# Loads and stores over 128 partitions in one transfer each, and another order of the first transfers, in a fused H3 and feed-forward kernel

## The chip, the cores and the metric

The kernel runs on one core of one Trainium2 chip. The metric is the device time of the whole program in microseconds, the median of several executions. The profile is of one execution; a span is the time from its first to its last instruction.

## The reference

For x of 2048 rows by 576 columns in float32, with xn the rows of x made zero-mean and unit-variance, the output is the sum of three parts:

```
xn  = (x - mean(x)) / sqrt(var(x) + 1e-5)
kv  = conv4(k, shift_k) * v                     # four taps along the sequence, causal, by channel
y   = causal_conv(kv, ssm_k) + kv * ssm_D       # 2048 taps, by channel; the reference goes by an FFT
out = x + xn * y + relu(xn @ w1) @ w2           # w1: 576 x 4608, w2: 4608 x 576
```

k and v are 2048 x 576, shift_k 576 x 4, ssm_k 576 x 2048, ssm_D 576. Everything is float32.

## The kernel before, in words

**Tiles.** A sequence position is p * 32 + u * 16 + t, with p below 64, u below 2, t below 16. Tile t holds 128 positions, one in each partition u * 64 + p, so a tile of x, k, v or out is two runs of 64 rows, each with a fixed step in DRAM, and the step from one run to the other differs. The function `move` (line 157) copies such a tile with one transfer for each u, over 64 partitions each. x is taken in pairs of tiles t, t+1, which lie next to each other in DRAM: 4608 bytes for each partition (`load_acc`, tile `acc`; a pair doubles as the accumulator of the output rows).

**Feed-forward part.** Four tiles are a block of 512 rows; there are four blocks. The hidden size is cut into 18 pairs of 128 columns. Matmuls are done in a rounded float32 (`F32R`), each operand split into a high and a low part and three of the four products summed. The columns of w1 come by `load_w1` into `both_w1` (named both_w in the profile): four groups of 128 rows, and the last 64 rows twice, in both halves of the partitions. `split_plain` and `split_rest` split them into `g` tiles; the high part is a copy on ACT (line 469), the low part a subtraction on POOL (line 431). w2 comes by `load_w2` into r (two buffers) and is split into w (line 531). Blocks 0 and 1 run against all pairs first, with plain products (`mm1`, line 569), then blocks 2 and 3 with a scheme of fewer products (`quad`, line 545). `unit` (line 632) multiplies by w2 and adds into acc.

**Opening.** `first_xT` centres the four tiles of block 0, tiles 0 and 2 on DVE (lines 179 to 200), tiles 1 and 3 on ACT (lines 254 and 256), transposes them on TensorE (line 262) and splits them into b1, b2 and xr (lines 221 to 227). Until then `keep_warm` runs matmuls on zeros (line 1112).

**Conv part.** `conv` is a generator; `tick`, called between the matmuls of the feed-forward part, advances it by its share. Its stages: the transform of ssm_k; that of kv, for which k and v are loaded two tiles ahead by `move` and the taps run on DVE (line 818 and around); a middle stage in DRAM tiles; and the output stage, which loads x again (tile xt), multiplies by it and, for the first eight tiles, stores to out from POOL's queue. The other eight tiles are stored from SP's queue out of acc (line 160), the last of them in halves (line 645).

**Order.** A scheduler lays out each engine's instructions from the program and its constraints (`issue_after`, `here`); each engine then runs its own in that order, and a waiting one holds those behind it. Transfers are issued from three queues: SP (q1 in the profile), ACT (q10) and POOL (q0).

Of the kernel before, what the change touches and what calls it, by code (L numbers as in the profile page):

```python
# [17 lines left out]
P = 128  # L18
# [22 lines left out]
NG = A1 // GR  # L41
N_WARM = 21
WARM_TILE = (0, 10, 0, 2)

# [65 lines left out]
def h3_ffn_kernel(ctx: ExitStack, tc, x, k, v, shift_k, ssm_k, ssm_D, w1, w2, fwd, inv, mid, out):  # L110
# [42 lines left out]
    def halves(u):  # L153

        return slice(u * A1, (u + 1) * A1), slice((1 - u) * A1, (2 - u) * A1)

    def move(tile_, rows, t, store=False, queues=(nc.sync, nc.sync)):
        for u in range(U):
            a, b = tile_[halves(u)[0]], rows[u, :, t]
            queues[u].dma_start(*((b, a) if store else (a, b)))  # L160

    pairs = {}

    def load_x(t, tag, bufs, late=False, **queues):
        pair = xp.tile([P, 2, D], F32, tag=tag, name=f"acc{t}", bufs=bufs)
        if late:
            with here():
                nc.vector.memset(pair[:, :, :1], 0.0)
        move(pair, x, slice(t, t + 2), **queues)
        return pair  # L170

    def load_acc(t, **queues):
        pairs[t] = load_x(t, f"acc{place(t // BT)}", BT // 2, **queues)
        acc[t], acc[t + 1] = pairs[t][:, 0, :], pairs[t][:, 1, :]
# [63 lines left out]
    def first_xT(srcs):  # L238
# [8 lines left out]
        for t in range(BT):  # L247
            xn = rows[t]
            if t % 2 == 0:
                with tc.issue_after(behind.ins) if behind else nullcontext():  # L250
                    stats(t, srcs[t])
                    behind = centred(xn, srcs[t], t)
            else:
                nc.scalar.activation(xn, srcs[t], AF.Copy, scale=-1.0 / D,
                                     accum_out=neg[:, t:t + 1])
                done["act"] = nc.scalar.activation(xn, srcs[t], AF.Identity,
                                                   bias=neg[:, t:t + 1])
                with tc.issue_after(done["act"].ins):
                    (split_plain if t == 1 else split_rest)(0, 0)
            for c in range(5):  # L260
                w = min(P, D - c * P)
                nc.tensor.transpose(ps[c][:w, t * P:(t + 1) * P], xn[:, c * P:c * P + w], ident)
            keep_warm(WARM_TILE[t])
        for c in range(5):
            last = split_low(c, ps[c], place(0))
            if c == 1:
                with tc.issue_after(last.ins):
                    split_plain(0, 1)
        with tc.issue_after(done["dve"].ins):
# [167 lines left out]
    def load_w1(n):  # L437
        f0 = (n % NPAIR) * FC
        r1 = both_w1[:, 5:] if n < NPAIR and n % 2 else both_w1
        for o, step in ((0, P), (P, FC - P)) if n == 0 else ((0, FC),):  # L440
            f, to = slice(f0 + o, f0 + o + step), slice(o, o + step)
            queue = nc.gpsimd if n == 0 and o == 0 else nc.sync
            queue.dma_start(r1[:, :4, to], w1[:4 * P, f].rearrange("(c p) f -> p c f", p=P))
            for h in range(2):
                queue.dma_start(r1[64 * h:64 * h + 64, 4, to], w1[4 * P:, f])
        raw_w[n] = r1
        weights[n] = {}
# [18 lines left out]

    def split_into(n, hi, lo, src):
        with at_turn(n):
            nc.scalar.activation(hi, src, AF.Copy)  # L469
        split_lo(lo, src, hi)  # L470

    def split_plain(n, j):
        g = weights[n][j] if j in weights[n] else group(n, j)
        weights[n][j] = g
        split_into(n, g[:, 0], g[:, 1], raw_w[n][:, :4, j * P:(j + 1) * P])

# [83 lines left out]
    def mm1(n, s, j):  # L560
# [3 lines left out]
        for c in range(4):  # L564
            b = ops[s, "b2" if c % 2 else "b1"][:, :, c // 2]
            seq += [(g[:, 0, c], b[:, 0]), (g[:, 0, c], b[:, 1]), (g[:, 1, c], b[:, 0])]
        seq += rest(n, j, s)
        for i, (a, m) in enumerate(seq):
# [46 lines left out]
    def unit(ns, s, b, i, h, last):  # L615
# [27 lines left out]
        if final and t == T - 1:  # L643
            for u, queue in ((0, nc.sync), (1, nc.scalar)):
                queue.dma_start(out[u, :, t, dc], acc[t][halves(u)[0], dc])
        elif last and h:
# [50 lines left out]
    def conv():  # L697
# [5 lines left out]
        with hold_pool as kp:  # L703
# [14 lines left out]
            def load(t):  # L718
                win[t] = slot(WIN + t % (KS + 1))
                if t >= 0:  # L720
                    move(win[t], k, t, queues=(nc.sync, nc.sync))
                    gates[t] = slot(GATE + t % 2)
                    move(gates[t], v, t, queues=(nc.sync, nc.sync))
                else:
# [257 lines left out]
        with tc.tile_pool(name="fo", bufs=2) as fp:  # L982
# [37 lines left out]
            def add(i):  # L1020
                if i >= 0:
# [5 lines left out]
                    if t < HT:  # L1027
                        move(to, out, t, store=True, queues=(nc.gpsimd, nc.gpsimd))
                    else:
                        added.add(t)  # L1030
# [70 lines left out]
    nc.vector.memset(warm, 0.0)  # L1101
    for t in range(0, BT, 2):
        load_acc(t, queues=(nc.sync, nc.scalar))
    load_w1(0)
# [14 lines left out]
    with tc.issue_after(done["act"].ins):  # L1119
        split_rest(0, 1)  # L1120
    load_w1(1)
    for t in range(BT, HT, 2):
        load_acc(t)
    for h in range(2):
        load_w2(0, h)
    for j in range(FT):
# [127 lines left out]
```

## Time and profile before

| | |
|---|---|
| median of 3 runs | 1058.05 us (1057.59 to 1059.14) |
| the profiled execution's own time | 1057.93 us |
| its span | 1056.2 us |
| TensorE busy | 1047.1 us, 99% of the span |
| DVE, ACT, POOL busy | 70%, 52%, 38% |
| moved by DMA | 204.45 MB, mean 194 GB/s |
| chain that ended last | PE 97%, DVE 1%, DMA 1% |

A row of the profile's groups or timeline has the start or the count, the engine, the line, the operation, output<-input and shapes; the part behind the bar or in brackets is idle time ahead of it and what ended it. A queue's row has its packets, MB, and the time of its packets as a share of sixteen DMA engines' time. A row of DMA issues has output<-input, the issuing queue, the count, KB of one and the median microseconds from issue to landing.

### The profile page before, as it was taken

The page shows a single profiled execution, that of the slowest core. Times are in us where ns is not written, and L with a number is a line of the kernel's source. Part 1 is how long each engine was busy: PE and PEld are TensorE (multiplying, and loading weights), DVE is VectorE, ACT ScalarE, POOL GpSimd, SP SyncE. Part 2 cuts the span into 40 slices and gives each one's busy share as a digit, 9 for nine tenths or more (in the row PEclk, how much of TensorE's full clock was granted, in tenths as well). Part 3 has the DMA queues.
Part 4 walks back from the last instruction along what each step waited for, and adds up shares of the span by engine and source line. Part 5 has one row for each costly group of instructions (what it writes and reads, how often), then busy time and mean ns, then how long its engine had stood idle before and what let it go on. Part 6 is the DMA issues. An engine that isn't in the chain of part 4 may idle for free.

```text
span 1056.2 us, 20042 instructions
## 1 busy us (share of the span) xinstructions
PE 1047.1 (99%) x7153; PEld 988.2 (94%) x7153; DVE 743.9 (70%) x1316; ACT 550.7 (52%) x1201; POOL 398.2 (38%) x398
## 2 busy tenths in 40 slices
PE   8999999999999999999999999999999999999998
PEld 5889999999999999999999999999999999999997
DVE  5539778787776788773477887778877773666664
ACT  5226566534343444433277787687777773444341
POOL 4133333333222333352443534343433444544641
PEclk9999999999999999999999999999999999999999
DMA  9944867777566766755876655656555648776864
GB/s 230 205 98 134 226 172 209 201 227 212 151 191 178 212 177 197 239 164 187 277 219 193 192 173 166 195 172 197 167 177 175 183 127 264 221 228 214 287 191 113
DMA packets 156304, 204.45 MB, mean 194 GB/s; under 512 B 32846, under 2 KB 122704, under 8 KB 155181
## 3 DMA queue, kind: packets, MB, share of 16 engines
q1 hardware_dynamic: 143308, 189.00, 60.5%
q0 software_dynamic: 12576, 13.44, 5.6%
q8 instruction: 56, 0.92, 0.4%
q10 hardware_dynamic: 320, 0.74, 0.3%
q14 instruction: 44, 0.35, 0.1%
HBM read 133.92 MB, written 55.05 MB: 179 GB/s over the span
## 4 chain that ended last, share of the span: by engine, by line
PE 97%; DVE 1%; DMA 1%; ACT 0%; issue 0%; SPq 0%; DVEq 0%
PE pso L632 43%; PE psh L569 22%; PE psb L545 14%; PE psf L907 7%; PE psa L545 6%; PE psf L687 3%; PE psf L1051 1%; PE psf L1053 1%; DMA acc<-in_x 1%; DVE bn L179 0%; PE psf L278 0%; ACT hh L551 0%; DVE lok L897 0%; DVE acc L641 0%; DVE yl L932 0%
## 5 line engine op out<-in xcount | busy, mean ns | idle before, releaser
L632 PE MATMUL pso<-w,hh 128*128 128x288 f32 x2304 | 468.9, 295 | 1.6 <-ACT w L531 0.8
L632 PEld LDWEIGHTS pso<-w,hh 128*128 128x128 f32 x2304 | 372.5, 188 | 9.8 <-ACT w L531 1.2
L632 PE MATMUL pso<-w,ll 128*128 128x288 f32 x1152 | 329.5, 295 | 0.0
L431 POOL TENSOR_TENSOR g<-both_w,g 128x256 fp32r<-128x256 f32 (+2 forms) x145 | 168.4, 1167 | 374.1 <-ACT g L469 322.4
L569 PE MATMUL psh<-b,g 128*128 128x512 f32 x864 | 218.2, 395 | 0.5 <-ACT b L226 0.2
L632 PEld LDWEIGHTS pso<-w,ll 128*128 128x128 f32 x1152 | 213.3, 188 | 1.1
L569 PEld LDWEIGHTS psh<-b,g 128*128 128x128 f32 x864 | 156.9, 188 | 30.5 <-DVE b L227 0.5
L641 DVE TENSOR_TENSOR acc<-pso,acc 128x288 f32<-128x288 f32 x232 | 101.7, 450 | 61.9 <-PE pso L632 59.1
L431 POOL TENSOR_TENSOR w<-r,w 128x576 fp32r<-128x576 f32 x72 | 113.0, 1570 | 53.8 <-ACT w L531 53.7
L551 ACT ACTIVATE hh<-psh 128x512 fp32r<-128x512 f32 x72 | 42.9, 597 | 143.8 <-PE psh L569 143.8
L552 DVE SCALAR_TENSOR_TENSOR ll<-psh,hh 128x512 fp32r<-128x512 f32 x72 | 49.4, 687 | 69.8 <-ACT hh L551 69.3
L545 PE MATMUL psb<-t,g 128*128 128x256 f32 x648 | 94.9, 280 | 0.1
L545 PEld LDWEIGHTS psb<-t,g 128*128 128x128 f32 x648 | 85.5, 188 | 0.4 <-DVE psa L600 0.3
L469 ACT ACTIVATE g<-both_w 128x256 fp32r<-128x256 f32 (+2 forms) x145 | 76.3, 543 | 9.9 <-PE psb L545 6.6
L498 POOL TENSOR_TENSOR both_w<-both_w 128x256 f32<-128x256 f32 x72 | 62.8, 891 | 30.3 <-DMA both_w<-in_w 29.0
L545 PE MATMUL psa<-b,g 128*128 128x256 f32 x432 | 63.1, 280 | 0.0
L551 ACT ACTIVATE hh<-psa 128x512 fp32r<-128x512 f32 x36 | 21.5, 598 | 72.9 <-PE psa L545 72.7
L545 PE MATMUL psb<-b,g 128*128 128x256 f32 x432 | 57.5, 281 | 0.0
L545 PEld LDWEIGHTS psa<-b,g 128*128 128x128 f32 x432 | 56.6, 188 | 0.0
L545 PEld LDWEIGHTS psb<-b,g 128*128 128x128 f32 x432 | 54.4, 188 | 0.2
L950 DVE TENSOR_TENSOR k<-psf,k 128x288 f32<-128x288 f32 x64 | 29.0, 454 | 35.1 <-ACT sw L949 33.3
L673 POOL DMA_DIRECT2D wx<-in_fwd x32 | 17.6, 551 | 95.3 <-PE psf L687 85.6
(135 smaller groups left out, 1695.3 us busy)
## 6 DMA issues: line engine op xcount, KB each, us to landing
r<-in_w SPq DMA_DIRECT2D x72, 288.0 KB, 4.0
zy<-vo SPq DMA_DIRECT2D x64, 288.0 KB, 2.9
zo<-zy SPq DMA_DIRECT2D x32, 576.0 KB, 4.4
both_w<-in_w SPq DMA_DIRECT2D x35, 512.0 KB, 4.2
zk<-zk SPq DMA_DIRECT2D x64, 144.0 KB, 2.6
ztk<-zk SPq DMA_DIRECT2D x32, 288.0 KB, 3.4
ztx<-zx SPq DMA_DIRECT2D x32, 288.0 KB, 3.5
k<-k SPq DMA_DIRECT2D x64, 144.0 KB, 3.3
```

The lines of the kernel that those rows point to most:

```text
L431: return nc.gpsimd.tensor_tensor(dst, src, hi, OP.subtract)
L469: nc.scalar.activation(hi, src, AF.Copy)
L498: nc.gpsimd.tensor_tensor(dst, a, b, op)
L545: done["pe"] = nc.tensor.matmul(ps, a, m, start=start and i == 0, stop=i == len(seq) - 1, skip_group_check=not start)
L551: done["act"] = nc.scalar.activation(hh, ps, AF.Relu)
L552: lows.append(nc.vector.scalar_tensor_tensor(ll, ps, 0.0, hh, op0=OP.max, op1=OP.subtract))
L569: done["pe"] = nc.tensor.matmul(ps, a, m, start=i == 0, stop=i == len(seq) - 1)
L632: done["pe"] = nc.tensor.matmul(ps[:, :NH], a, m, start=c == 0, stop=c == len(seq) - 1)
L641: done["acc"] = nc.vector.tensor_tensor(acc[t][:, dc], ps[:, :NH], acc[t][:, dc], OP.add)
L687: nc.tensor.matmul(ps[:, :NH], w[:, n, :], stk, start=n == 0, stop=n == 1)
L907: nc.tensor.matmul(ps[:, :NH], a, m[:, cols], start=n == 0, stop=n == 2)
L950: nc.vector.tensor_tensor(k1[:, cols], ps, k1[:, cols], OP.mult)
```

## The change

`move` makes one transfer of a whole tile: the tile's 128 partitions on one side, `rows[:, :, t]` with u and p as its two outer dimensions on the other. The last 64 rows of w1 come by one transfer too, from a source that names them twice. The first pair of x is issued from ACT's queue, the second from SP's; the first tile of w1 from both of these in halves and no longer from POOL. Its high part is split after both centrings on ACT, and the second tile's high part is copied on POOL. The loads of w2 for pair 0 are issued ahead of block 1's x. There are 23 warm-up matmuls where there were 33, and the first twelve matmuls of block 0 take another order. The last tile's stores are split by columns, not by partitions.

```diff
-N_WARM = 21
-WARM_TILE = (0, 10, 0, 2)
+N_WARM = 20
+WARM_TILE = (0, 2, 0, 1)
...
-    def move(tile_, rows, t, store=False, queues=(nc.sync, nc.sync)):
-        for u in range(U):
-            a, b = tile_[halves(u)[0]], rows[u, :, t]
-            queues[u].dma_start(*((b, a) if store else (a, b)))
+    def move(tile_, rows, t, store=False, queue=nc.sync):
+        a, b = tile_, rows[:, :, t]
+        done["move"] = queue.dma_start(*((b, a) if store else (a, b)))
...
-                with tc.issue_after(done["act"].ins):
-                    (split_plain if t == 1 else split_rest)(0, 0)
+                if t == BT - 1:
+                    with tc.issue_after(done["act"].ins):
+                        split_plain(0, 0)
...
-            if c == 1:
+            if c == 2:
                 with tc.issue_after(last.ins):
-                    split_plain(0, 1)
+                    split_rest(0, 0)
+        split_plain(0, 1, nc.gpsimd.tensor_copy)
...
-            queue = nc.gpsimd if n == 0 and o == 0 else nc.sync
-            queue.dma_start(r1[:, :4, to], w1[:4 * P, f].rearrange("(c p) f -> p c f", p=P))
-            for h in range(2):
-                queue.dma_start(r1[64 * h:64 * h + 64, 4, to], w1[4 * P:, f])
+            cuts = ((nc.scalar, 0, 2), (nc.sync, 2, 4)) if n == 0 and o == 0 else ((nc.sync, 0, 4),)
+            for queue, a, b in cuts:
+                queue.dma_start(r1[:, a:b, to],
+                                w1[a * P:b * P, f].rearrange("(c p) f -> p c f", p=P))
+            nc.sync.dma_start(r1[:, 4, to], w1[4 * P:, f][None].to_broadcast([2, 64, step]))
...
+        if n == 0 and s == place(0):
+            seq = [seq[i] for i in (0, 3, 1, 2, 6, 4, 5, 9, 7, 8, 10, 11)]
...
-            for u, queue in ((0, nc.sync), (1, nc.scalar)):
-                queue.dma_start(out[u, :, t, dc], acc[t][halves(u)[0], dc])
+            (nc.scalar if h else nc.sync).dma_start(out[:, :, t, dc], acc[t][:, dc])
...
-                    move(win[t], k, t, queues=(nc.sync, nc.sync))
+                    move(win[t], k, t)
                     gates[t] = slot(GATE + t % 2)
-                    move(gates[t], v, t, queues=(nc.sync, nc.sync))
+                    move(gates[t], v, t)
...
-                        move(to, out, t, store=True, queues=(nc.gpsimd, nc.gpsimd))
+                        move(to, out, t, store=True, queue=nc.gpsimd)
...
-    for t in range(0, BT, 2):
-        load_acc(t, queues=(nc.sync, nc.scalar))
+    for t, queue in ((0, nc.scalar), (2, nc.sync)):
+        load_acc(t, queue=queue)
...
+    for h in range(2):
+        load_w2(0, h)
     for t in range(BT, HT, 2):
         load_acc(t)
-    for h in range(2):
-        load_w2(0, h)
```

SP's queue at the start, before and then in the changed kernel. acc0, acc2, acc4 and acc6 are the pairs of x (0 and 2 of block 0, 4 and 6 of block 1), both_w1 is w1, r2_n_h is half h of w2 for pair n; the shape is that of the written side.

```order
L160 DMA acc0_97<-in_x 64x1152
L160 DMA acc2_100<-in_x 64x1152
L443 DMA both_w1_94<-in_w1 128x4x128
L445 DMA both_w1_94<-in_w1 64x128 x2
L443 DMA both_w1_94<-in_w1 128x4x256
L445 DMA both_w1_94<-in_w1 64x256 x2
L160 DMA acc4_229<-in_x 64x1152 x2
L160 DMA acc6_232<-in_x 64x1152 x2
L452 DMA r2_0_0_235<-in_w2 128x2x288
L452 DMA r2_0_1_237<-in_w2 128x2x288
```

```order
L445 DMA both_w1_94<-in_w1 128x2x128
L159 DMA acc2_99<-in_x 128x1x1152
L447 DMA both_w1_94<-in_w1 128x1x128
L445 DMA both_w1_94<-in_w1 128x4x128
L447 DMA both_w1_94<-in_w1 128x1x128
L445 DMA both_w1_94<-in_w1 128x4x256
L447 DMA both_w1_94<-in_w1 128x1x256
L454 DMA r2_0_0_215<-in_w2 128x2x288
L454 DMA r2_0_1_217<-in_w2 128x2x288
L159 DMA acc4_219<-in_x 128x1x1152
L159 DMA acc6_221<-in_x 128x1x1152
```

Half of the first w1 tile now stands ahead of x's second pair on SP, w2 of pair 0 ahead of block 1's x. In both, two loads of ssm_D, w1 of pairs 2 and 3 and then r2_1_0 follow; ACT's queue holds the two other halves of x before, and acc0 and the other half of the first w1 tile in the changed kernel.

SP's queue in the transform of kv, a stretch with the loads of one tile (k and v are inputs, both the area they land in, xs and zx the conv's own transfers):

```order
L160 DMA both_345<-in_k 64x576 x2
L160 DMA both_345<-in_v 64x576 x2
L867 DMA zx_85<-both_345 128x288
L414 DMA kept_xr_93<-rows2_679 128x512
L867 DMA zx_85<-zx_2226 128x288
L841 DMA xs1_0_2897<-both_345 64x576
L841 DMA xs1_1_2898<-both_345 64x576
```

```order
L159 DMA both_329<-in_k 128x1x576
L159 DMA both_329<-in_v 128x1x576
L873 DMA zx_85<-both_329 128x288
L415 DMA kept_xr_93<-rows2_660 128x512
L873 DMA zx_85<-zx_2198 128x288
L847 DMA xs1_0_2864<-both_329 64x576
L847 DMA xs1_1_2865<-both_329 64x576
```

The order is the same; two transfers became one for k and one for v. The end of SP's queue, the stores of the last eight tiles:

```order
L160 DMA out_0<-acc8_6146 64x1152 x2
L160 DMA out_0<-acc10_6200 64x1152 x2
L160 DMA out_0<-acc12_5879 64x1152 x2
L160 DMA out_0<-acc14_5927 64x576 x2
L645 DMA out_0<-acc14_5927 64x288 x2
```

```order
L159 DMA out_0<-acc8_6073 2x64x1152
L159 DMA out_0<-acc10_6126 2x64x1152
L159 DMA out_0<-acc12_5809 2x64x1152
L159 DMA out_0<-acc14_5856 2x64x576
L651 DMA out_0<-acc14_5856 2x64x288
```

Each pair of stores is one, and the last tile's two SP stores are one, its second columns going from ACT.

More of the change, by code (lines that the diff above doesn't have):

```diff
@@ L155, in halves, with load_x @@
         return slice(u * A1, (u + 1) * A1), slice((1 - u) * A1, (2 - u) * A1)
-    def move(tile_, rows, t, store=False, queues=(nc.sync, nc.sync)):
-        for u in range(U):
-            a, b = tile_[halves(u)[0]], rows[u, :, t]
-            queues[u].dma_start(*((b, a) if store else (a, b)))
+    def move(tile_, rows, t, store=False, queue=nc.sync):
+        a, b = tile_, rows[:, :, t]
+        done["move"] = queue.dma_start(*((b, a) if store else (a, b)))
     pairs = {}
-    def load_x(t, tag, bufs, late=False, **queues):
+    def load_x(t, tag, bufs, late=False, **queue):
         pair = xp.tile([P, 2, D], F32, tag=tag, name=f"acc{t}", bufs=bufs)
@@ L168, in load_x, with load_acc @@
                 nc.vector.memset(pair[:, :, :1], 0.0)
-        move(pair, x, slice(t, t + 2), **queues)
+        move(pair, x, slice(t, t + 2), **queue)
         return pair
-    def load_acc(t, **queues):
-        pairs[t] = load_x(t, f"acc{place(t // BT)}", BT // 2, **queues)
+    def load_acc(t, **queue):
+        pairs[t] = load_x(t, f"acc{place(t // BT)}", BT // 2, **queue)
         acc[t], acc[t + 1] = pairs[t][:, 0, :], pairs[t][:, 1, :]
@@ L465, in group, with split_into, split_plain @@
         return wp.tile([P, 2, 4, P], F32R, tag="g", name=f"g{n}_{k}", bufs=4)
-    def split_into(n, hi, lo, src):
+    def split_into(n, hi, lo, src, copy=None):
         with at_turn(n):
-            nc.scalar.activation(hi, src, AF.Copy)
+            if copy:
+                copy(hi, src)
+            else:
+                nc.scalar.activation(hi, src, AF.Copy)
         split_lo(lo, src, hi)
-    def split_plain(n, j):
+    def split_plain(n, j, copy=None):
         g = weights[n][j] if j in weights[n] else group(n, j)
         weights[n][j] = g
-        split_into(n, g[:, 0], g[:, 1], raw_w[n][:, :4, j * P:(j + 1) * P])
+        split_into(n, g[:, 0], g[:, 1], raw_w[n][:, :4, j * P:(j + 1) * P], copy)
     def rest_flat(n):
```

## The prediction

> **What bounds the kernel now.** I read the page's busy times first, then the busy times by stage, then the queues and the DMA issues of each stage. TensorE is busy from the first microsecond to the last few:
>
> ```profile
> span 1056.2 us, 20042 instructions
> ...
> PE 1047.1 (99%) x7153; PEld 988.2 (94%) x7153; DVE 743.9 (70%) x1316; ACT 550.7 (52%) x1201; POOL 398.2 (38%) x398
> ...
> q1 hardware_dynamic: 143308, 189.00, 60.5%
> q10 hardware_dynamic: 320, 0.74, 0.3%
> ...
> 0.00:62.00 62.00, 57.95 (x312) 45.96 (x313) 28.84 (x75) 21.49 (x42) 18.40 (x23) 1.00 0.82 194
> 62.00:198.00 136.00, 136.00 (x822) 123.89 (x821) 103.84 (x194) 75.22 (x171) 47.41 (x56) 1.00 0.65 174
> 198.00:446.00 248.00, 248.00 (x1489) 225.32 (x1487) 193.12 (x307) 99.69 (x199) 76.26 (x75) 1.00 0.70 199
> 500.00:550.00 50.00, 50.00 (x386) 49.47 (x385) 26.98 (x53) 25.00 (x57) 19.02 (x20) 1.00 0.84 266
> 580.00:876.00 296.00, 295.91 (x2261) 292.09 (x2260) 230.74 (x402) 221.80 (x497) 120.62 (x103) 1.00 0.59 175
> 876.00:1041.00 165.00, 165.00 (x1267) 162.89 (x1266) 102.52 (x194) 65.51 (x151) 83.25 (x92) 1.00 0.72 224
> 1041.00:1056.00 15.00, 10.24 (x77) 9.91 (x75) 5.35 (x12) 0.60 (x1) 0.00 (x0) 0.98 0.60 157
> ```
>
> In the stage rows the columns are length, busy time of PE, PEld, DVE, ACT, POOL, granted clock, DMA share and GB/s. So what a change wins outside the opening and the last store must come off TensorE's own work, and this one takes none off. What it can lose is another matter: the last columns say that the sixteen DMA engines are already 0.59 to 0.84 busy. The conv's matmuls stand in TensorE's one queue between those of the feed-forward part, so a conv transfer that is late holds everything.
>
> **How a transfer is spread over engines.** The queue rows tell it. ACT's queue (q10) carries four transfers: two of 64 rows of x, two of 64 rows of out, 256 pieces. Its row has 320 packets, 64 more: each transfer closes with 16 packets, one for each engine. SP's program has 800 transfers that come to 130,559 pieces; with 16 closing packets each that is 143,359. The row has 143,308, which is 51 fewer. Five transfers are not of 64 or more rows: two loads over one row (ssm_D) and three over 63 (k, line 726). One engine for a single row is 15 fewer, twice, and nine engines of seven rows for 63 is 7 fewer, three times: 30 + 21 = 51. So engines are given equal shares of the outermost count; 63 rows use nine engines, not sixteen unevenly.
>
> In the changed kernel the DRAM side of every load of x, k and v and of every store of out is `rows[:, :, t]`, whose outermost dimension is u, of count 2; the tile's side has 128. The last 64 rows of w1 become a broadcast whose outermost count is 2 also. Equal shares on both sides at once are possible for two engines only. By the tile's side alone it would be sixteen; the transfers of before with unlike sides (32 against 128 rows, 256 against 128) have 16 in common and don't decide. I take two, and, as the simplest deal, one from the first engine on, the same two each time, so that all these transfers queue there.
>
> [...]
>
> **What a byte costs on one engine.** Two stretches bound it, one in which the output stage loads 128-row pieces and one in which block 1's x is loaded by halves:
>
> ```profile
> q1 hardware_dynamic: 189, 0.80, 99.8%
> q1 hardware_dynamic: 293, 1.08, 104.2%
> ```
>
> The first is 879 to 881 us: 0.80 MB / (2.0 us x 16 x 0.998) = 25 GB/s for an engine. The second is 12.5 to 17 us: 1.08 / (4.5 x 16 x 1.042) = 14.4 GB/s. I take 25, because two engines that draw 50 GB/s together are nearer to engines that nothing else slows; 14.4 is the other end. A pair of x tiles, 295 KB to each of two engines, is then 11.8 us, k or v of one tile 5.9 us, the rest of a w1 load 2.6 us.
>
> **The opening.** Until the second pair's w2 (r2_1_0 in SP's order) one engine of the two has, on its rings: four x pairs 4 x 295, the first w1 tile 16, its rest and the second tile 33 + 16 + 33, w1 of pair 1 33 + 66, two halves of w2 37, w1 of pairs 2 and 3 2 x 98, r2_1_0 itself 18: 1.63 MB. At 25 GB/s that is 65 us, from a start near 2 (the first x issue) to 67, plus 0.7 for the split of w2. Now:
>
> ```profile
> 0.76 1.23 ACTq L160 DMA_DIRECT2D acc<-in_x  x2
> 1.21 8.66 PE L1112 MATMUL psw<-warm 128*128 128x512 bf16 x33 [1.21 <-DVE table L1106]
> 9.36 0.63 ACT L469 ACTIVATE g<-both_w 128x512 fp32r<-128x512 f32 x1 [1.59 <-DMA both_w<-in_w]
> 9.82 0.82 DVE L179 BATCH_NORM_STATS2 bn<-acc 128x6 f32<-128x288 f32 x2 [2.01 <-DMA acc<-in_x]
> 10.07 1.28 POOL L431 TENSOR_TENSOR g<-both_w,g 128x512 fp32r<-128x512 f32 x1 [6.39 <-ACT g L469]
> 13.28 0.50 PE L569 MATMUL psh<-b,g 128*128 128x512 f32 x1 [0.25 <-ACT b L226]
> 26.00 0.69 ACT L531 ACTIVATE w<-r 128x576 fp32r<-128x576 f32 x1
> 30.32 0.69 PE L632 MATMUL pso<-w,hh 128*128 128x288 f32 x4
> ```
>
> The split at 26.00 is that of r2_1_0, and the matmuls that need it start at 30.32. They come at 68 instead: +38 us. The first real matmul (13.28), with x whole near 27, would be late by 16, which lies inside the 38. That w2 is issued ahead of block 1's x spares pair 0 the 24 us of those two loads; pair 1's w2 still stands behind them, on SP's queue, with w1 of pairs 2 and 3 behind x as well. At 14.4 GB/s the opening is 113 us long, +85.
>
> The other parts of the opening edit are covered by this wait: ten fewer warm-up matmuls, the g split behind the centring, the cast of the second tile on POOL (nearest row 10.07: 1.28 us for a 128x512 subtraction there), the new order of twelve matmuls. None of them can be read in the end time while x is late; with x early they cost what the first rival below charges.
>
> **The conv of x, 198 to 446 us.**
>
> ```profile
> both<-in_k SPq DMA_DIRECT2D x35, 144.0 KB, 4.5
> both<-in_v SPq DMA_DIRECT2D x30, 144.0 KB, 3.2
> both_w<-in_w SPq DMA_DIRECT2D x18, 64.0 KB, 3.5
> rows<-in_x SPq DMA_DIRECT2D x4, 288.0 KB, 4.1
> ```
>
> Of the 35, 32 are moved (the other three keep their 64 rows). Moved: 62 x 144 + 18 x 64 + 4 x 288 KB = 11.5 MB, 29 us of each of sixteen engines now and 230 us of each of two after. All traffic now takes 0.70 x 248 = 174 us of an engine; 174 - 29 + 230 = 375, against 248: +127. The taps wait for k within the same tile, so the load can't be put off past the stage. If part of the 0.70 is packets held up by each other and 25 GB/s is the whole price, 199 x 248 / 16 / 25 = 123 takes the place of 174, the load is 324 and the stage +76.
>
> **Block 2's x, 500 to 550 us.** Eight halves of x (the rows are the issues at 517 and 540 us) and four rests are 2.6 MB, 52 us in place of 6.6 on top of 0.84 x 50 = 42: 88, +38 if all is awaited there and 0 if the slacker stretch behind it takes it up. I take +25, since acc waits for them directly. In 62 to 198 us (four halves of x rows and eight rests, 1.7 MB) the load becomes 88 + 30 = 118 of 136, and in 580 to 876 (eighteen rests) 175 + 21 of 296: nothing in either.
>
> **The output stage and the last stores, 876 to the end.**
>
> ```profile
> xt<-in_x SPq DMA_DIRECT2D x32, 144.0 KB, 3.8
> out<-y POOLq DMA_DIRECT2D x16, 144.0 KB, 4.5
> both_w<-in_w SPq DMA_DIRECT2D x10, 64.0 KB, 4.8
> out<-acc SPq DMA_DIRECT2D x6, 288.0 KB, 3.5
> 1041.30 10.36 SPq L160 DMA_DIRECT2D out<-acc  x8
> 1051.75 1.43 SPq L645 DMA_DIRECT2D out<-acc  x2
> ```
>
> With the single tile and the last halves, out<-acc is 2.4 MB and the moved part on SP and ACT 7.7 MB: 19 us now, 155 after. 0.72 x 165 + 0.60 x 15 = 128 now; 128 - 19 + 155 = 264 of 180: +83. That holds the tail, where the last stores alone, 3 x 11.8 + 5.9 + 5.9 = 47 us of one engine, start at 1041 and have nothing behind which to hide. POOL's stores of y, if on the same two engines, add 41; I leave them out, as another queue.
>
> **The sum.** 38 + 127 + 25 + 83 = 273. The profiled execution is 1057.93 us, its span 1056.2; 1057.9 + 273 = 1331. That execution is 0.1 below the median of the three runs, 1058.05, so the forecast is 1330.
>
> **Rivals.** *Sixteen engines all the same* (the tile's 128 rows decide): then the change does what it says. For it: the two halves share one set of engines now, and the output stage's 128-row loads run at 399 GB/s where block 1's x runs at 240. The x pairs and the half of the first tile ahead of them, 1.31 MB, then take 3.3 to 5.5 us from 2, so x is whole at 5.3 to 7.5 in place of 9.8, and 23 warm-up matmuls end at 1.2 + 23/33 x 8.66 = 7.2. The first matmul comes 2.3 to 4.5 us sooner, less 0.6 for the first tile's split, which now follows the centring on ACT (row 9.36), and TensorE carries that to the end: 2.8 in the middle, 1055.2. Against it: 63 rows on nine engines. [...]
>
> *Two engines, but others each time*: each transfer is long, none queues. x 11.8 us, the opening +5; k lands 8 us after issue where 4.5 was, 2.5 late at each of 16 tiles, +40; the last pair's store +7. 1110. Nothing in the rows ties a transfer to an engine, nor the reverse.
>
> *Two engines at 14.4 GB/s*: the opening +85, the conv 174 - 29 + 400 = 545, +297, the rest twice its sum, +220: about 1660. For it the second rate row; against it that sixteen engines drew that together.
>
> **How the numbers follow.** Forecast 0.70, sixteen engines 0.12, changing engines 0.10, the slow rate 0.08. The forecast's own range is 1225 (38 for the opening, 76 for the conv, 0 for block 2, and 54 for the end by the same reckoning: 168) to 1480 (POOL's stores on top, and stalls in which the two engines run dry between tiles, some 100); the whole range reaches down to 1100 and up to 1500. A measurement of this kernel tells 0.2%, 2.1 us, from no change. Faster by that is 0.6 of the first rival, 0.07; same 0.04; slower 0.89.
>
> **What would show it.** Right: q1 has 140,710 packets (130,943 pieces and 9,767 closings, two for each of the 101 moved transfers) and q10 532; x is whole near 27 us; DVE waits for DMA on k in the conv; TensorE's busy share falls to near 80%, and the DMA share sinks while the span grows; the out stores end some 40 us after the last matmul. Wrong: 142,124 packets on q1, 560 on q10 and x landing before 9 us say sixteen engines; x near 14 us says two that change; 1600 says the rate.

## The result: 27% slower, and the profile after

The changed kernel takes 1340.75 us (median of 5 runs, 1337.87 to 1342.3) against 1058.05: a ratio of 1.2667, 95% interval [1.2649, 1.2684]. The forecast was 1330, its range 1100 to 1500. The profiled execution is the median one, its span 1339.0.

Rows of the page of the changed kernel (engines, then queues with packets, MB and share of sixteen engines' time):

```profile
span 1339.0 us, 19867 instructions
...
PE 1102.0 (82%) x7143; PEld 1032.6 (77%) x7143; DVE 743.4 (56%) x1316; ACT 549.9 (41%) x1200; POOL 390.6 (29%) x388
...
q1 hardware_dynamic: 140710, 189.19, 46.1%
q0 software_dynamic: 15888, 13.14, 4.4%
...
q10 hardware_dynamic: 532, 0.87, 0.2%
```

Both packet counts are those of two engines, to the packet (140,710 and 532; sixteen would have been 142,124 and 560). SP's queue moves what it moved before, 189 MB, and its packets take 46.1% of a longer span: 9,876 us of engine time, where 60.5% of 1056.2 was 10,224. By these figures the engines do no more work than before; by the packets it lies on fewer of them.

Where the time went is read by following the same matmul through both traces. Behind the warm-up each has 7,120 matmuls, and but for 18 places among the first 96, where the order was changed, they come in the same order; the n-th of one answers to the n-th of the other. The boundaries that the prediction used fall in the changed kernel at 107.4, 251.8, 599.0, 665.6, 779.8 and 1075.4 us, and the last matmul ends at 1299.4. Busy times by stage there (length, busy PE, PEld, DVE, ACT, POOL, granted clock, DMA share, GB/s):

```profile
0.00:107.40 107.40, 63.87 (x302) 51.31 (x303) 28.51 (x75) 20.96 (x41) 16.77 (x21) 0.78 0.41 112
107.40:251.80 144.40, 138.35 (x823) 125.72 (x822) 104.02 (x194) 75.15 (x171) 47.63 (x56) 0.98 0.58 164
251.80:599.00 347.20, 267.14 (x1488) 239.97 (x1487) 193.17 (x307) 100.47 (x201) 77.00 (x76) 0.89 0.47 141
599.00:665.60 66.60, 57.52 (x323) 52.09 (x323) 28.78 (x42) 18.32 (x36) 19.48 (x18) 0.91 0.49 153
665.60:779.80 114.20, 90.96 (x616) 88.34 (x615) 49.86 (x93) 46.91 (x104) 30.50 (x31) 0.90 0.50 164
779.80:1075.40 295.60, 295.60 (x2262) 292.13 (x2261) 231.48 (x402) 221.83 (x497) 120.34 (x103) 1.00 0.60 175
1075.40:1299.40 224.00, 188.53 (x1340) 183.00 (x1339) 107.09 (x204) 66.30 (x152) 78.93 (x84) 0.92 0.53 167
1299.40:1339.00 39.60, 0.01 (x1) 0.00 (x0) 0.46 (x1) 0.00 (x0) 0.00 (x0) 0.56 0.12 50
```

The rows answer to 62, 136, 248, 54, 80, 296 and 175 us of the kernel before, and the last to the 4.9 us behind its last matmul. Only the sixth has no loss: of the changed transfers it holds only the last rows of w1, and joined alone (e4 below) they cost nothing there. The last row shows the two engines bare: TensorE does nothing, SP's and ACT's stores are all that is left, the DMA share is 0.12 (2 of 16 is 0.125) and 50 GB/s flow.

The opening, from the timeline of the changed kernel (start, length, what it waited for):

```profile
2.61 20.59 SPq L445 DMA_DIRECT2D both_w<-in_w  x1
...
24.03 0.82 DVE L178 BATCH_NORM_STATS2 bn<-acc 128x6 f32<-128x288 f32 x2 [22.88 <-DMA acc<-in_x]
...
27.11 0.69 ACT L253 ACTIVATE xn<-acc 128x576 f32<-128x576 f32 x1 [1.50 <-DMA acc<-in_x]
...
31.01 5.42 PE L576 MATMUL psh<-b,g 128*128 128x512 f32 x15
...
72.41 0.68 ACT L536 ACTIVATE w<-r 128x576 fp32r<-128x576 f32 x1 [28.67 <-DMA r<-in_w]
73.14 0.85 PE L639 MATMUL pso<-w,hh 128*128 128x288 f32 x2 [15.69 <-ACT w L536]
```

x is whole at 27.1, the first real matmul starts at 31.0, and the matmuls with the second pair's w2 at 73.1 in place of 30.3. The first row is SP itself: issuing one load of w1 takes it 20.6 us.

What TensorE waited for longest in the changed kernel (total, times, longest):

```profile
PE psf L693 <- DMA xs<-both: 74.1, 10, 27.9
PE pso L639 <- DVE acc L648: 20.5, 5, 8.3
PE psf L1057 <- DMA zo<-zy: 19.5, 8, 9.0
```

Neither xs nor zo is a transfer that was changed. Both stand on SP's queue behind ones that were (k and v ahead of xs, xt ahead of zo). The longest of these waits ends at 378.8 us. Its xs was issued only at 369.8, and ahead of that ACT had waited 22.8 us for zx, a transfer that was not changed either.

### The profile page after: what moved, and what is told of

Read it like the earlier page. It is cut to its first block, busy times and chain, and to the rows that moved or that the text cites. A ratio compares the mean times of both kernels' runs of the same rounds, so it can differ in the third digit from the quotient of the medians.

```text
span 1339.0 us, 19867 instructions
## 1 busy us (share of the span) xinstructions
PE 1102.0 (82%) x7143; PEld 1032.6 (77%) x7143; DVE 743.4 (56%) x1316; ACT 549.9 (41%) x1200; POOL 390.6 (29%) x388
## 3 DMA queue, kind: packets, MB, share of 16 engines
q1 hardware_dynamic: 140710, 189.19, 46.1%
q0 software_dynamic: 15888, 13.14, 4.4%
## 4 chain that ended last, share of the span: by engine, by line
PE 58%; DMA 23%; SPq 9%; issue 3%; DVE 2%; POOL 1%; ACT 1%; DVEq 0%; POOLq 0%; ACTq 0%
PE pso L639 26%; PE psh L576 12%; PE psb L550 8%; DMA zo<-zy 6%; PE psf L913 5%; DMA xs<-both 4%; PE psa L550 4%; DMA acc<-in_x 4%; SPq L445 3%; PE psf L693 2%; DMA both_w<-in_w 1%; SPq L873 1%; DMA kept_t<-area 1%; SPq L1016 1%; DMA nrm<-rows 1%
## 5 line engine op out<-in xcount | busy, mean ns | idle before, releaser
L639 PE MATMUL pso<-w,hh 128*128 128x288 f32 x2304 | 492.6, 306 | 38.0 <-DVE acc L648 20.5
L639 PEld LDWEIGHTS pso<-w,hh 128*128 128x128 f32 x2304 | 392.3, 198 | 48.6 <-DVE acc L648 22.2
L639 PE MATMUL pso<-w,ll 128*128 128x288 f32 x1152 | 340.3, 304 | 0.0
L639 PEld LDWEIGHTS pso<-w,ll 128*128 128x128 f32 x1152 | 224.1, 197 | 1.2
L693 PE MATMUL psf<-xs,wx 128*128 128x288 f32 x128 | 30.5, 321 | 76.7 <-DMA xs<-both 74.1
L503 POOL TENSOR_TENSOR both_w<-both_w 128x256 f32<-128x256 f32 x72 | 60.4, 857 | 98.2 <-DMA both_w<-in_w 96.9
L693 PEld LDWEIGHTS psf<-xs,wx 128*128 128x128 f32 x128 | 23.1, 201 | 82.2 <-issue 50.1
L474 ACT ACTIVATE g<-both_w 128x512 fp32r<-128x512 f32 (+1 forms) x144 | 75.8, 542 | 25.2 <-POOL both_w L503 17.2
L536 ACT ACTIVATE w<-r 128x576 fp32r<-128x576 f32 x72 | 48.5, 674 | 35.1 <-DMA r<-in_w 35.1
L694 ACT ACTIVATE both<-psf 128x288 f32<-128x288 f32 x43 | 17.6, 408 | 104.0 <-DMA zx<-both 55.5
L644 DVE SCALAR_TENSOR_TENSOR acc<-pso,rstd,acc 128x288 f32<-128x288 f32 x72 | 36.5, 510 | 41.7 <-PE pso L639 41.4
```

The lines of the kernel that those rows point to most:

```text
L503: nc.gpsimd.tensor_tensor(dst, a, b, op)
L536: nc.scalar.activation(t[:, 0], r2, AF.Copy)
L639: done["pe"] = nc.tensor.matmul(ps[:, :NH], a, m, start=c == 0, stop=c == len(seq) - 1)
L693: nc.tensor.matmul(ps[:, :NH], w[:, n, :], stk, start=n == 0, stop=n == 1)
```

## The experiments

All are compared with the kernel before, run on the same chip between them (1058.2 each time). The stage table below is worked out for each as above: by how much the same matmul starts later than in the kernel before, the growth from one boundary to the next, in us; "behind" is what the time behind the last matmul grew by, and the sum is that of the spans, to rounding. A rest is a load of the last 64 rows of w1, and x's rows are the loads of x in the transform of kv. "Forecast" is the prediction's sum.

```
                          0-62  62-198 198-446 446-500 500-580 580-876 876-end of PE  behind   sum
forecast                    38       0     127       0      25       0      83 (both)          273
changed kernel            45.4     8.3    99.2    12.7    34.2    -0.4          48.8    34.7  282.8
e1  twice 64 everywhere   -2.3     0.0     0.0     0.0     0.0    -0.4           0.3    -0.1   -2.5
e2  count 16              -0.7     0.0     0.0     0.0     0.0    -0.1           1.1    -0.3   -0.1
e3  k, v joined           -1.9     1.2    59.9    10.6     0.0    -0.1           0.1    -0.1   69.7
e4  rest of w1 joined     12.1     0.0     0.0     0.2     3.0    -0.5           0.2     0.6   15.4
e5  last stores joined    -2.4     1.1     0.0     0.0     0.0    -0.1           0.3    34.4   33.3
e6  x of blocks 0, 1      34.2     0.0     0.0     0.0     1.0    -0.2           0.2     0.0   35.2
e7  count 4               16.6     0.1    17.1     7.3    11.8    -0.6           7.1    15.7   75.0
e8  xt joined             -2.5     0.5     0.0     0.0     0.0    -0.1          40.8    -0.2   38.4
e9  x of blocks 2, 3      -0.7     0.0     0.0     0.0    30.0    -0.2           0.3     0.1   29.4
e12 k, v, rest, rows      12.1    10.6    98.2    12.8     1.8    -0.5           0.2     0.3  135.5
```

**e1: two transfers of 64 again, the opening edit kept.**

```diff
-        a, b = tile_, rows[:, :, t]
-        done["move"] = queue.dma_start(*((b, a) if store else (a, b)))
+        for u in range(U):
+            a, b = tile_[halves(u)[0]], rows[u, :, t]
+            queue.dma_start(*((b, a) if store else (a, b)))
...
-            (nc.scalar if h else nc.sync).dma_start(out[:, :, t, dc], acc[t][:, dc])
+            for u in range(U):
+                (nc.scalar if h else nc.sync).dma_start(out[u, :, t, dc], acc[t][halves(u)[0], dc])
...
-            nc.sync.dma_start(r1[:, 4, to], w1[4 * P:, f][None].to_broadcast([2, 64, step]))
+            for h in range(2):
+                nc.sync.dma_start(r1[64 * h:64 * h + 64, 4, to], w1[4 * P:, f])
```

> The changed kernel with every tile again moved by two transfers of 64 partitions, the last 64 rows of w1 too; its other edits (queues and order of the first transfers, centring, 23 warm-up matmuls, cast on POOL) stay. Theory (the outermost count of 2 puts a transfer on two engines): all 283 us go, since nothing else of the change touches the stages behind the opening; what is left is the opening edit alone, 1053 to 1060. Rival (the new order of the first transfers, or w2 ahead of block 1's x, is a part of the loss): 15 us or more stay, 1073 and above. SP's queue should have 143,740 packets (130,943 pieces, 12,797 closings).

Measured: 1055.58 us, ratio 0.9980 [0.9971, 0.9989]. The whole loss is gone and 2.5 us are won; the queue's row and the first real matmul of e1:

```profile
q1 hardware_dynamic: 143740, 189.20, 61.0%
```

```profile
12.47 4.01 PE L578 MATMUL psh<-b,g 128*128 128x512 f32 x15 [0.25 <-ACT b L226]
```

So the loss sits in the joined transfers, none of it in the order of the first loads; that order, with the rest of the opening edit, is worth 2.5 us by itself. This kernel is faster than both.

**e2: one transfer a tile, outermost count 16.** x, k, v and out get a second view, used by the moves alone (the loads of single shifted rows of k keep theirs); the last rows of w1 go by two loads of 64. A tile then holds other rows of the sequence, so the result is not that of the reference; only the time is of use.

```diff
+UM = 16
...
+    x_m = x[0].rearrange("(p u t) d -> u p t d", u=UM, t=T)
...
-        move(pair, x, slice(t, t + 2), **queue)
+        move(pair, x_m, slice(t, t + 2), **queue)
```

> The changed kernel with one transfer of 128 partitions for each tile as it has, but the rows of a tile taken as 16 runs of 8 (one in each partition as before, other rows of the sequence, so that the output's rows are those of another sequence order): the outermost count of the DRAM side is 16 in place of 2, bytes, partitions, queues and number of transfers stay. The last 64 rows of w1 go by two transfers of 64. Theory: sixteen engines again, 1052 to 1060, and 142,716 packets on SP's queue, 560 on ACT's. Rival (a transfer over 128 partitions that is one is slow by itself, whatever its outermost count): 1290 to 1341, and the packets 141,820 and 532. This run also gives what the change would bring if the sixteen engines carried it: the prediction's first rival said 1055.2.

Measured: 1055.86 us, 0.9980 [0.9972, 0.9989]. The queues of e2:

```profile
q1 hardware_dynamic: 142716, 189.20, 61.1%
...
q10 hardware_dynamic: 560, 0.87, 0.3%
```

With sixteen runs of 8 rows in place of two of 64, and the tile's side, bytes, partitions, queues and number of transfers as in the changed kernel, nothing is lost. So it is not the transfer over 128 partitions that was slow here (1055.86), but the count of 2 (1340.75). And one such transfer is no faster than two of 64 either: 1055.86 against 1055.58.

**e7: outermost count 4.** As e2 with `UM = 4`.

> As the kernel with 16 runs of 8 rows, but a tile taken as 4 runs of 32 (the output's rows again those of another sequence order): outermost count 4. Theory (engines = count): 141,948 packets on SP's queue and 536 on ACT's; the loads take half of what two engines take: opening x 24 us of an engine, +10; kv 174 - 26 + 103 = 251 of 248, +6; output stage 128 - 19 + 77 = 186 of 180, +6; last stores 24 us, +10: 1088 (1070 to 1100). Rival (any count below 16 costs the same as 2): 1320 or more; (4 is enough to spread): 1056.

Measured: 1133.04 us, 1.0705 [1.0687, 1.0723]. The queues of e7, and the stretch in which only stores are left:

```profile
q1 hardware_dynamic: 141948, 189.19, 56.4%
...
q10 hardware_dynamic: 536, 0.87, 0.3%
```

```profile
1111.00:1126.00 15.00, 0.00 (x0) 0.00 (x0) 0.11 (x1) 0.00 (x0) 0.00 (x0) 0.64 0.26 94
```

Four engines, to the packet, and 0.26 of sixteen busy (4 of 16 is 0.25) at 94 GB/s: the equal shares hold for a third count. The price was too low: +77 over e1 where +32 was reckoned. The table shows where: 11.8 us between 500 and 580 us and 7.3 between 446 and 500, for which nothing was charged, 17.1 for 6 in the transform of kv, 19 for 10 in the opening, 15.7 for 10 behind the last matmul. The reckoning compared an engine's load with the stage's length; with four engines the load, so reckoned, fits nearly everywhere, and the waits come all the same (15.5 us of TensorE's for xs).

**e3 to e6, e8, e9, e12: one group of transfers joined, everything else as in e1.** `move` gets a `join` that picks the changed kernel's form, set at the calls named:

```diff
+        if join:
+            a, b = tile_, rows[:, :, t]
+            queue.dma_start(*((b, a) if store else (a, b)))
+            return
...
-                    move(win[t], k, t)
+                    move(win[t], k, t, join=True)
...
-                    move(gates[t], v, t)
+                    move(gates[t], v, t, join=True)
```

*e3, k and v.*

> Only k and v are moved by one transfer a tile (count of 2); x, out and the last rows of w1 go by transfers of 64. Theory: the loss is that of the transform of kv alone. The prediction's reckoning for that stage was +127 with x's rows and w1's rest in it; without them k and v are 9.1 MB, 23 us of each of sixteen engines or 184 of each of two at 25 GB/s: 174 - 23 + 184 = 335 of 248, +87, so 1145 (lower end, packets held up by each other: +40, 1098). Nothing in the opening, after 600 us, or in the last stores. Rival (two engines, but others for each transfer, none queues behind another): 2.5 us at each of 16 tiles, +40, 1098, with DMA waits spread evenly over the tiles; if the stage's loss came from x's rows, 1060. SP's queue: 142,780 packets.

Measured: 1127.64 us, 1.0656 [1.0642, 1.0671]: +72 over e1, 59.9 in the stage and 10.6 behind it. That lies between the theory's 1145 and the 1098 of the rival, so this run alone does not tell them apart; e5 and e6 do. TensorE's longest wait in e3:

```profile
PE psf L700 <- DMA xs<-both: 39.6, 9, 8.0
```

It is not k that TensorE waits for by this row, but xs, a transfer on all sixteen engines (16 closing packets, as for every unchanged transfer of 64 rows or more in the changed kernel's 140,710) that SP issues behind the next tiles' k and v: on two of the sixteen it stands behind 5.9 us of k and 5.9 of v (an estimate at 25 GB/s for an engine). The trace bears it out: two of these nine waits end at 421.5 and 527.7 us, for pairs of xs that were issued by 414.4 and 519.5, so 7 to 8 us from issue to landing, where the median in e1 is 2.7.

*e4, the last rows of w1:*

```diff
-            for h in range(2):
-                nc.sync.dma_start(r1[64 * h:64 * h + 64, 4, to], w1[4 * P:, f])
+            nc.sync.dma_start(r1[:, 4, to], w1[4 * P:, f][None].to_broadcast([2, 64, step]))
```

> Only the last 64 rows of w1 go by one transfer whose source names them twice (count of 2); all tiles go by transfers of 64. Theory: 64 KB on each of two engines, 2.6 us of each for a pair of weights whose turn is some 14 us in the first half: hidden behind the opening, within 3 us of the kernel that has twice 64 everywhere. SP's queue: 142,630 packets. Rival (the source that repeats itself is slow in its own right, or these loads share in the loss): 20 us or more above it.

Measured: 1072.51 us, 1.0131 [1.0115, 1.0146]: +17, 14.4 of it in the opening. Neither expectation was right. Four pairs' rests are loaded there, each 64 KB on one engine, 2.6 us by the prediction's price: 10.5 for four, most of the 14.4. In the opening there is no slack to hide that: from 10 to 50 us in e1 all sixteen engines are full, a share of 1.02:

```profile
10.00:50.00 40.00, 39.02 (x227) 33.64 (x226) 25.41 (x66) 14.71 (x29) 12.86 (x12) 1.00 1.02 240
```

*e5, the stores of the last eight tiles from SP and ACT:*

```diff
-                move(acc[t], out, t, store=True)
+                move(acc[t], out, t, store=True, join=True)
...
-                move(pairs[t - 1], out, slice(t - 1, t + 1), store=True)
+                move(pairs[t - 1], out, slice(t - 1, t + 1), store=True, join=True)
...
-            for u in range(U):
-                (nc.scalar if h else nc.sync).dma_start(out[u, :, t, dc], acc[t][halves(u)[0], dc])
+            (nc.scalar if h else nc.sync).dma_start(out[:, :, t, dc], acc[t][:, dc])
```

> Against the kernel of twice 64 everywhere (1055.6): only the stores of the last eight tiles to out from SP and ACT are one transfer each (count of 2). Theory (the two engines are the same ones each time, so transfers queue): these stores are 47 us of one engine, and hardly any lies ahead of 1039, where the pairs come ready: they end near 1086, so 1089 (1080 to 1095), TensorE's last matmul where it was, and while only stores are left 50 GB/s and a DMA share of 0.12. Rival (other engines each time): the last pair and its halves overlap, +7, 1063, at 100 GB/s or more.

Measured: 1091.48 us, 1.0314 [1.0298, 1.0329]: +36. In e5 the last matmul is where it was; behind it:

```profile
1054.00:1089.50 35.50, 0.00 (x0) 0.00 (x0) 0.00 (x0) 0.00 (x0) 0.00 (x0) 0.50 0.12 49
```

Several stores are under way at once, from two queues, and together they get two engines' worth. So it is the same two each time, for SP and for ACT; other engines each time would show as a larger share.

*e6, x of blocks 0 and 1:*

```diff
-        load_acc(t, queue=queue)
+        load_acc(t, queue=queue, join=True)
...
-        load_acc(t)
+        load_acc(t, join=True)
```

> Against the kernel of twice 64 everywhere (1055.6): only the four pairs of x of blocks 0 and 1 are one transfer each. Theory: 47 us of each of two engines at 25 GB/s in place of 6 of each of sixteen, in a stretch in which the engines are full already (DMA share 1.02 to 1.05 from 10 to 50 us, 0.18 from 50 to 60): +41 less the 8 of slack, +33, 1089; at most the whole +41, 1097. x of block 0 is whole near 25 us and the first real matmul at 28. Rival (the loads run beside each other on different engines): x whole at 14, 1061.

Measured: 1092.55 us, 1.0327 [1.0311, 1.0342]: +37. From the timeline of e6:

```profile
25.77 0.87 PE L267 MATMUL psf<-ident,xn 128*128 128x128 f32 x3 [17.51 <-DVE xn L204]
...
31.17 4.36 PE L582 MATMUL psh<-b,g 128*128 128x512 f32 x15
```

The transposes start at 25.8 as in the changed kernel (25.8) and not at 14, as engines that change would have it.

*e8, the output stage's loads of x:*

```diff
-                    move(xt, x, t)
+                    move(xt, x, t, join=True)
```

> Against the kernel of twice 64 everywhere (1055.6): only the output stage's loads of x (xt, 16 tiles) are one transfer each. Theory: 94 us of each of two engines in place of 12 of each of sixteen: 128 - 12 + 94 = 210 of 180 from 876 us to the end, +30, 1086; if part of the stage's DMA share is packets held up by each other, the load is under 180 and the loss 0 to 10. This splits the changed kernel's 49 us between 876 us and the last matmul into xt's share and that of POOL's stores of y. Rival (other engines each time): 2 us late at each tile at most, +0 to +10, spread evenly.

Measured: 1096.71 us, 1.0367 [1.0352, 1.0382]: +41, all between 876 us and the last matmul. TensorE's waits in e8:

```profile
PE psf L1064 <- DMA zo<-zy: 16.9, 7, 4.2
PE psf L1064 <- DVE y L1069: 11.1, 1, 11.1
```

Again a bystander, zo, is what TensorE waits for. That leaves 8 us of the changed kernel's 49 for POOL's stores of y and for the rests of w1 in that stage (five pairs, 13 us of each of the two engines by count, but no loss alone, in e4). Neither was run together with xt, so the two are not told apart.

*e9, x of blocks 2 and 3 (`acc_loads`):*

```diff
-                load_acc(t, late=True)
+                load_acc(t, late=True, join=True)
```

> Against the kernel of twice 64 everywhere (1055.6): only the four pairs of x of blocks 2 and 3, which acc waits for between 500 and 580 us, are one transfer each. By load alone: they are 47 us of each of two engines in place of 6; 0.84 x 50 + 0.58 x 30 = 59 now, 100 after in a stretch of 80, +20, 1076. Rival (what is awaited directly costs its own time at two engines, whatever the stage has to spare): the changed kernel lost 34 between 500 and 580 us, 1090. If others of the changed kernel's transfers on the same two engines made that loss: under 10, 1065.

Measured: 1087.59 us, 1.0275 [1.0261, 1.0289]: +32, close to the rival's 34. Waits between 490 and 620 us of e9:

```profile
DVE acc L654 <- DMA acc<-in_x: 32.8, 4, 10.4
```

Four pairs, four waits, up to 10.4 us where a pair on two engines takes 11.8 (an estimate at 25 GB/s for an engine): this is the time of single transfers, awaited directly, not a stage that is full. It is also what e7 paid between 500 and 580 us: there DVE waits 14.8 us for the same four loads, up to 4.7 each, where a pair on four engines takes 5.9 by the same estimate.

*e12, all that the changed kernel joins in the transform of kv: k, v, the last rows of w1, x's rows for blocks 2 and 3* (on e3):

```diff
-                     slice(b * BT + i, b * BT + i + 2))
+                     slice(b * BT + i, b * BT + i + 2), join=True)
...
-            for h in range(2):
-                nc.sync.dma_start(r1[64 * h:64 * h + 64, 4, to], w1[4 * P:, f])
+            nc.sync.dma_start(r1[:, 4, to], w1[4 * P:, f][None].to_broadcast([2, 64, step]))
```

> Against the kernel of twice 64 everywhere (1055.6): k and v, the last rows of w1 and the rows of x in 62 to 198 and 198 to 446 us are one transfer each, what the changed kernel joins in the transform of kv, and nothing of x's pairs, xt or out. In 198 to 446 us k and v alone lost 60 where the changed kernel lost 99; 18 rests of 64 KB for each of two engines (47 us by count, 23 of them in this stage) and 4 halves of x's rows (24 us) are to account for the other 39. Theory (load on the same two engines adds up): +99 in 198 to 446 us, +11 behind it, and 17 for the rests in the opening and near 550: 1055.6 + 72 + 39 + 17 = 1184 (1170 to 1195). Rival (they are hidden there, and the 39 came from work that was late for other reasons): 1145 or less.

Measured: 1191.87 us, 1.1253 [1.1234, 1.1272]. 98.2 us in the stage where the changed kernel has 99.2, 12.8 behind it where that has 12.7. The 39 us that k and v alone left open fit the load of the rests and rows on the same two engines: 24 and 24 by count, less the 6 that they took of each engine before. The loss between 62 and 198 us is that of x's rows: the rests alone (e4) cost 0.0 there, and the waits name the rows. In the changed kernel, between 107.4 and 251.8 us:

```profile
DVE bn L178 <- DMA rows<-in_x: 5.3, 1, 5.3
```

```profile
PE psf L693 <- DVE ks L686: 6.0, 2, 3.1
```

DVE stands 5.3 us for a load of rows, what it owes to TensorE comes late, and TensorE stands 6.0; the stage's matmuls take some 2 us longer, at a granted clock of 0.98. e12 has the same two waits (5.3 and 5.6), and 1.2 for POOL's load of wk, a wait that e5 and e11 have too (0.8 and 1.4) and that the change did not make.

**Adding up.** Over e1: e5 35.9, e6 37.0, e8 41.1, e9 32.0, e12 136.3, together 282.3. With e1's 1055.58 that is 1337.9; the changed kernel has 1340.75. That it comes so near is in part luck. The 2.9 us left hold POOL's stores, the one group not run alone, and what the groups do to each other, and these have both signs: by the table the groups alone come to 3 us more than the changed kernel in the opening and to 8 less in the output stage.

**e10 and e11: the opening edit, on e1.** e10 puts w2 of pair 0 behind block 1's x again:

```diff
-    for h in range(2):
-        load_w2(0, h)
     for t in range(BT, HT, 2):
         load_acc(t)
+    for h in range(2):
+        load_w2(0, h)
```

> The kernel of twice 64 everywhere (1055.6), with w2 of pair 0 issued behind block 1's x again. If this edit carries a part of the 2.6 us that the opening edit won: w2 lands 1.18 MB / 263 GB/s = 4.5 us later, the matmuls with it (19.3 us) wait: +1.2 to +3.5, 1056.8 to 1059. Rival (w2 is early enough either way, the gain is the earlier x and first w1 tile alone): within 0.4 of 1055.6.

Measured: 1055.91 us, 0.9979 [0.9970, 0.9987]. Within 0.4 of e1: this part of the edit brings nothing that can be measured.

e11 splits both of block 0's pairs over the two queues by halves, ahead of w1's first tile:

```diff
-    for t, queue in ((0, nc.scalar), (2, nc.sync)):
+    for t, queue in ((0, (nc.sync, nc.scalar)), (2, (nc.sync, nc.scalar))):
```

> The kernel of twice 64 everywhere (1055.6), with each pair of block 0's x split over SP's and ACT's queues by halves and the two halves of the first w1 tile behind both. x's second pair lands in front of 131 KB of w1 instead of behind it: 0.5 to 0.9 us sooner, 1054.7 to 1055.1. Rival (w1's first tile is then the last to land and ends the wait): 1055.4 to 1056.

Measured: 1057.42 us, 0.9998 [0.9989, 1.0007]: slower than either expectation. The first real matmul comes at 11.33, 1.1 sooner than in e1, and the matmul that started at 30.1 before is 3.2 us early, but at 62 us 1.7 of that are left and at 130 us nothing. e11's DMA from 10 us on:

```profile
10.00:50.00 40.00, 37.95 (x217) 32.50 (x216) 23.81 (x63) 13.61 (x28) 12.83 (x12) 1.00 1.03 229
50.00:60.00 10.00, 10.00 (x52) 8.54 (x52) 1.60 (x3) 2.54 (x5) 3.28 (x3) 1.00 0.34 88
```

The engines are as full as in e1 and move less (229 GB/s for 240), and 50 to 60 us still has work (e1: 0.18). The same bytes must come in that stretch; which reordering costs the 11 GB/s is not shown.

## Why the prediction was right, step by step

**Two engines.** The step that decided the sign held exactly: equal shares of the outermost counts of both sides. In the runs, counts of 2, 4 and 16 against 128 give the packets of 2, 4 and 16 engines (140,710, 141,948 and 142,716 on SP's queue). It had been read out of 51 missing packets of the kernel before, on 63-row and one-row loads. Other counts below 16 were not run against 128. The prediction also took the two to be the same each time, one from the first engine on, as the simplest deal. That they are the same e5 shows (0.12 of sixteen busy and 49 GB/s with several stores under way); which of the sixteen they are no run shows.

**25 GB/s for an engine.** 50 GB/s on two in the changed kernel's last row, 49 in e5. The other end, 14.4, was block 1's x among other traffic, and its rival fell.

**The opening, +38: too small.** x whole at 27 held (27.1), and so did the place of the loss, the wait for r2_1_0; its size did not: 68 forecast, 73.1 measured, 42.8 of the 45.4. The sum took r2_1_0 to land when the two engines have done the bytes ahead of it. The last packets of x do end by 60 us. But SP issues r2_1_0 only then, and loads of ssm_k, which the sum does not have, right behind it (from 63.9). From 67 to 72, with r2_1_0 still on its way, not two but all sixteen engines are busy, 0.91 of the time:

```profile
60.43 3.37 SPq L454 DMA_DIRECT2D r<-in_w  x2
```

```profile
67.00:72.00 5.00, 0.00 (x0) 0.00 (x0) 0.00 (x0) 0.00 (x0) 0.00 (x0) 0.50 0.91 188
```

The other 2.6 us come behind the wait without a further one for DMA: up to 76 us the granted clock is 0.50 and a matmul that took 0.29 us takes 0.44. By runs, the 45.4 are -2.3 (e1), 36.5 (e6 over e1) and 14.4 (the rests, e4 over e1), which do not quite add.

**62 to 198 us, 0: wrong by 8.3.** A load of 118 in 136 was called no loss, and by load there is room; but DVE waits directly for x's rows (e12 above).

**The conv, +127: too large.** 99.2, and 12.7 more in the stretch behind it. The slope of the term was right (the rests and rows, 40 by its load, cost 38 between e3 and e12); the base was not. k and v alone were to take 335 us of an engine and took 308. If load is all that counts there, the engine's 174 us before were 147 of load and 27 of packets held up by each other; that is argued from the sum, not shown. The prediction had the two ends, 174 and 123, and took the upper one.

**Block 2's x, +25: 34.2.** Its bounds, 0 and 38, hold it; e9 puts 30.0 of it on these loads, and e4 3.0 on the rests. The term was reckoned as load on a stage, and it is four waits for four transfers.

**580 to 876 us, 0:** -0.4, as the slack said.

**The output stage and last stores, +83:** 48.8 + 34.7 = 83.5, but not by the prediction's parts. xt alone cost 41 where load against length gave 30; most of TensorE's waits there are for zo (16.9 us in e8), which stands behind 5.9 us of xt (an estimate at 25 GB/s for an engine), so that waits for single transfers come on top of the load. That reading is argued from the rows, not run. The last stores' 47 us of one engine cost 34.7 of what was, by the forecast, inside the 83. POOL's stores, left out at 41 if they shared the engines, have with the rests the other 8.

So the sum, 273 against 282.8 by the spans, is closer than its terms: -7 and -8 in the opening and behind it, +15 in the conv, -9 at block 2. The mechanism was right, the two engines and their rate; that the time came within 11 us is in part luck, since these errors cancel.

**The rivals.** Sixteen engines would have given 1055.2: e2, which is that case, measured 1055.86. Two that change (1110) are excluded by e5's row for the stores and by e6 for the loads of x; the slow rate (1660) by e5's 49 GB/s.

**What would show it.** All signs came. DVE does wait for k in the conv, between 251.8 and 600 us of the changed kernel:

```profile
DVE both L821 <- DMA both<-in_k: 7.5, 1, 7.5
DVE both L824 <- DMA both<-in_k: 6.9, 1, 6.9
```

What the signs did not have is the larger wait, TensorE's 74.1 us for xs.

## What to carry to other kernels

Before two transfers are joined into one, look at the outermost dimension that the joined access has on each side: with two runs of 64 rows it was 2 here, and the tile's 128 partitions did not help (1340.75 us, where a count of 16 with the same 128 partitions took 1055.86). In these runs the closing packets on SP's and ACT's queues told how many engines a transfer had, without timing anything: 2 and 4 for each joined transfer in the changed kernel and e7, and 0.12 and 0.26 of sixteen busy where only stores were left. On POOL's they did not: its 89 transfers close with 1,424 packets, 16 each, in the changed kernel and in e2 alike. When transfers sit on a few engines, price two things: their load against the stage's length, and, for each one that an engine waits for directly, its own length (e9: waits of up to 10.4 us). The second cost also fell on unchanged transfers that were issued behind: xs took 7 to 8 us to land in two waits of e3, where its median in e1 is 2.7.

## What the runs showed that was not expected

**The issuing queue stops.** SP took 20.59 us to issue one w1 load in the opening (in e1 the same row takes 0.39); none of its buffers had been used before. In e6, where only x is joined, the issue of two such loads takes 18.70; in e7, with x on four engines, 10.91. So in these runs the issue of an unchanged load is long where x's packets ahead of it are on a few engines, and longer with two than with four; what holds SP there no run shows. The prediction had no term for it.

**POOL's queue has more packets, not fewer.** From POOL the changed kernel stores y in 8 transfers with a count of 2, and its queue has 15,888 packets where e1 has 12,432 and e2 12,304. The trace's packets of that queue hold 3,584 of 8 bytes, none in e1 or e2, and 1,536 in e7: 8 x 14 x 32 and 8 x 12 x 16. The data are 512 packets of 4,608 bytes in all three, 64 a transfer: 32 for each of two engines, or 16 for each of four. The small packets are as many as if each of the other 14 or 12 engines got one for every large packet of an engine with data; the trace does not say which engine a packet was on, so that is a reading of the counts. The median from issue to landing, changed kernel and e2:

```profile
out<-y POOLq DMA_DIRECT2D x8, 288.0 KB, 10.3
```

```profile
out<-y POOLq DMA_DIRECT2D x8, 288.0 KB, 4.5
```

The loss, 8 us with that of the rests, is far from the 41 us of the prediction's case of shared engines. Which engines these transfers were on no run here shows.

**TensorE also slows.** Its busy time grew by 56 us over e1 (1102.0 against 1045.9) for the same matmuls, at a mean granted clock of 0.91; the first 15 took 5.42 us behind the wait for x where e1 took 4.01. The prediction had no term for it. The idle time grew by 229 us (237.0 against 7.8), so the slow matmuls are 56 us of the loss at most. They come in the stages with waits (granted clock 0.78 to 0.98 by the stage rows; 1.00 in the sixth, which has no loss); what of the 56 would be left if they ran at full clock, and the waits were longer for it, was not separated.
